# A new written order for a squared-ReLU attention and token/channel mixer kernel on one core

## The chip, the core and the metric

The kernel runs on one core of a Trainium2 chip. A core has five engines that run their own instruction streams and meet through semaphores: TensorE (PE, matrix products, and PEld, its weight loads), VectorE (DVE), ScalarE (ACT), GpSimd (POOL) and SyncE (SP). Data moves between memory and the core by DMA transfers; here POOL issues the loads of inputs and weights, and SP (at the end ACT too) issues the stores and the transposes that are done by DMA. Products land in PSUM, which has eight banks of 128 x 512 floats; everything else stands in SBUF. The metric is the device time of one execution in microseconds (us), lower being better.

## What is computed

Eight batches, twelve heads, 448 tokens, 64 numbers per head. The attention has no softmax: scores are clipped at zero and squared. Its output goes through a mixer over tokens and one over channels.

```python
def _attn_ref(q, k, v):                       # (8, 12, 448, 64)
    scores = scale * np.matmul(q, k.transpose(0, 1, 3, 2))
    attn = np.maximum(scores, 0.0) ** 2 / S
    return np.matmul(attn, v).astype(np.float32)
...
def _moe_ref(x, w_tok1, w_tok2, w_ch1, w_ch2):  # x (8, 448, 768)
    xt = x.transpose(0, 2, 1)
    h = np.maximum(xt @ w_tok1, 0.0) @ w_tok2   # 448 -> 256 -> 448
    u = x + h.transpose(0, 2, 1)
    h2 = np.maximum(u @ w_ch1, 0.0) @ w_ch2     # 768 -> 1536 -> 768
    return (u + h2).astype(np.float32)
```

## The kernel before

**Tiles.** The attention runs in 24 steps, three to a batch, four heads to a step; the four heads lie as two halves of two. Keys are cut into 7 tiles of 64 tokens. For every step the kernel does:

- `T`: PE transposes k and q against an identity matrix (line 472), 56 products of 64x64, one set for each half in steps 0 to 2 and further on partly for both halves; `cp` copies them out of PSUM (ACT or DVE, lines 349 and 351). From step 10 on, a crossing takes their place: DVE copies k and q, and SP transposes them by DMA (line 497).
- `S s.c`: the scores of key tile c, four products of 64x64 weights and 448 columns into two banks (line 515); `r` clips each bank into SBUF (ACT line 343 or DVE line 345), `q` squares both (ACT line 355 or DVE line 357).
- `V s.c`: the value products, again groups of four with 64x64 weights (line 542), summed over the seven tiles in two banks; `xe` empties these.
- The token mixer: `X` (PE transposes, line 579; from step 6 on SP does it by DMA, line 566), `t1` (line 588), its clipping `rt`, `t2` (line 597), and the addition `u` of x on DVE (line 601). These work on whole 128x128 tiles.

Per batch, `C1` (line 623) and `C2` (line 713) are the channel mixer of the earlier batches; `M1` (line 780) and `M2` (line 847) are products of pre-added weights and activations that take the place of some of its products, with additions and snapshots on DVE and ACT. SP transposes u into `u_sb` by DMA (`ub b.g`, line 610), six for each batch, and the last additions (`d2`, lines 860 and 862) read it before the stores `st` (line 668).

**Small and whole tiles.** `T`, `S` and `V` use PE as 64x64 tiles, all other products the whole 128x128 array. A run of small-tile operations between whole-tile ones is called a stretch here.

**Order.** Nothing is scheduled by a tool. All operations are built first, under names as above, and then issued one after the other as a table of words, `ORDER` (lines 73 to 242), says. A word is a name, and behind the colon stands what is left to choose: `:A` or `:D` sets ACT or DVE, digits set the PSUM banks of a product, and for a POOL load a name makes that load wait for another operation too. `fill:4*5` is a product of a zero tile whose result nothing reads, here one of 512 columns (5 // 4) and one of 128 (5 % 4) into bank 4. The order of the words is the order in which each engine meets its instructions.

```python
for word in ORDER.split():
    name, _, how = word.partition(':')
    ...
    o = self.ops[name]
    assert name not in done and all((d.name in done for d in o.deps)), name
    ...
    if how in ('A', 'D'):
        o.on = 'ACT' if how == 'A' else 'DVE'
    ...
    else:
        o.bank = [int(k) for k in how]
    o.emit(o)
```

**Loads.** POOL issues the halves of k, q and v (`ldk s.half` and so on, line 371, 112 KB each); a buffer is free again four steps later. The first q comes from SP and ACT (`ldf`, line 424) and is cast by DVE and ACT. The token weights are `wt1` and `wt2` (lines 382 and 389), the large channel weights `wc1.0` to `wc1.2` and `wc2.0` to `wc2.2` (lines 397 and 406), six parts of 768 KB. The identity matrix (`ident`, line 434) is made on POOL as well. The first two DMA transposes of u, `ub0.0` and `ub0.1`, are held until `wc2.2` has landed (`hold`).

Of the kernel before, what the change touches and what calls it, by code (L numbers as in the profile page):

```python
# [74 lines left out]
T0.0:0 ldv0.1 T0.1:1 cp0.0:D ldv0.0 cp0.1:D ldq2.0 ldk2.0 fill:4*5 S0.3:23
S0.1:45 S0.6:67 r0.3.0:A r0.3.1:D ldq2.1 S0.5:01 r0.1.0:A r0.1.1:D S0.0:23 wt1.1 r0.6.0:A r0.6.1:D r0.0.0:A
ldv1.1 q0.1:D r0.0.1:A ldk2.1 q0.3:D r0.5.0:A T1.0:45 r0.5.1:A q0.0:D S0.4:67 ldq3.0 S0.2:23 cp1.0:A cp1.1:D
ldk3.0 q0.5:D V0.0:01 r0.2.0:A S1.2:54 V0.1 q0.6:D r0.2.1:A ldv1.0 r0.4.0:A r0.4.1:D S1.3:23 ldv2.1 r1.2.0:A
q0.2:D r1.2.1:A wt1.0 q0.4:D r1.3.0:A V0.2 S1.1:67 ldv3.0 V0.3 q1.2:D r1.3.1:A V0.4 S1.4:54 r1.1.0:A ldk4.1
r1.1.1:D S1.0:23 r1.4.0:A r1.4.1:D ldk3.1 S1.6:67 r1.0.0:A V0.5 V0.6 q1.1:D r1.0.1:A ldk4.0 xe0.1:D xe0.0:A  # L80
ldq3.1 r1.6.0:A T2.0:54 q1.0:D r1.6.1:A q1.3:D X0.0:2 wt2 X0.1:3 cp2.0:A cp2.1:D S1.5:01 V1.0:67 ldq5.0 V1.1
q1.4:D r1.5.0:A V1.2 S2.3:45 ldq4.1 V1.3 r1.5.1:A xc0.0:D V1.4 xc0.1:D r2.3.0:A ldk5.1 S2.0:02 q1.5:D r2.3.1:A
S2.2:13 ldv4.0 q1.6:D r2.0.0:A fill:4*3 V1.5 S2.1:45 r2.0.1:A r2.2.0:D ldq6.1 r2.1.0:A r2.1.1:D S2.6:02 V1.6
ldv3.1 r2.2.1:A t1.0.0:1 q2.0:D xe1.0:A ldq5.1 S2.4:45 xe1.1:D r2.6.0:A V2.0:36 r2.6.1:A q2.1:D X1.1:0 ldq4.0
rt0.0:A q2.2:D r2.4.0:A fill:7*2 V2.1 S2.5:72 ldk6.0 q2.3:D r2.4.1:A V2.2 T3.0:14 r2.5.0:A xc1.1:D ldv5.0 V2.3
q2.4:D r2.5.1:A t2.0.0:5 cp3.0:A ldk5.0 cp3.1:D t1.1.1:0 X1.0:7 u0.0:D wc1.0 rt1.1:A V2.4 S3.2:24 xc1.0:A
q2.5:D t2.1.1:1 r3.2.0:A q2.6:D ldq6.0 S3.1:50 r3.2.1:A u1.1:D S3.4:72 ldk6.1 V2.5 r3.1.0:A V2.6 q3.2:D ub0.3
t1.1.0:4 r3.1.1:A ldv4.1 xe2.1:D xe2.0:A S3.0:15 wc1.2 t1.0.1:0 r3.4.0:A r3.4.1:D X2.1:6 rt1.0:A q3.1:D X2.0:3
r3.0.0:A wc2.0 S3.3:72 xc2.1:D rt0.1:A r3.0.1:A T4.0:41 xc2.0:D wc1.1 q3.4:D r3.3.0:A S3.6:60 t2.0.1:3
r3.3.1:A cp4.0:D t1.2.1:5 wc2.2 r3.6.0:A u0.1:D S3.5:72 r3.6.1:A cp4.1:D t1.2.0:4 rt2.1:A t2.1.0:6 r3.5.0:A  # L90
q3.0:D t2.2.1:3 rt2.0:A q3.3:D r3.5.1:A S4.1:05 S4.4:17 u1.0:D r4.1.0:A V3.0:42 V3.1 u2.1:D r4.1.1:A ub0.2
S4.3:60 V3.2 r4.4.0:A q3.5:D V3.3 S4.0:53 r4.4.1:A V3.4 r4.3.0:D ldk7.0 t2.2.0:1 r4.3.1:A ub0.5 q3.6:D V3.5
r4.0.0:A T5.0:76 u2.0:D r4.0.1:A ldq7.0 S4.2:05 V3.6 q4.1:D cp5.0:A ub0.4 C1.0.3:1 ldk7.1 xe3.1:D xe3.0:A
cp5.1:D ldv5.1 r4.2.0:A C1.0.1a:3 q4.0:D r4.2.1:A c1e0.3:A q4.3:D S4.6:72 S4.5:46 V4.0:05 q4.2:D r4.6.0:A V4.1
C1.0.1 r4.5.0:A r4.5.1:D C1.0.2a:1 r4.6.1:A q4.4:D c1e0.1:A C1.0.2 q4.5:D T6.0:74 q4.6:D c1e0.2:A S5.5:62 V4.2
cp6.0:A cp6.1:D V4.3 V4.4 ldq7.1 V4.5 r5.5.0:D S5.3:31 r5.5.1:A V4.6 S6.3:47 r5.3.0:A r5.3.1:D X3.0:6 xe4.0:A
xe4.1:D C1.0.9:2 r6.3.0:A r6.3.1:D xc3.0:A q5.3:D C1.0.10:3 q5.5:D c1e0.9:A q6.3:D wc2.1 X4.0:1 c1e0.10:A
S6.0:05 xc4.0:D S6.4:47 S6.1:62 r6.0.0:A C1.0.11:3 r6.0.1:A r6.4.0:D r6.1.0:A r6.4.1:D r6.1.1:A S5.4:10 q6.0:D
S5.6:54 c1e0.11:A S5.2:67 q6.1:D t1.4.0:2 r5.4.0:A q6.4:D r5.4.1:A t1.3.0:3 r5.6.0:A r5.2.0:D r5.6.1:A
r5.2.1:D ldv7.1 C1.0.8:1 rt4.0:A q5.4:D rt3.0:A q5.2:D S5.1:05 q5.6:D c1e0.8:A S6.5:64 w1.0.0:D S5.0:72  # L100
r5.1.1:D C1.0.5:3 r5.0.1:A r5.0.0:A w1.0.2:D r5.1.0:A t2.4.1:1 C1.0.6:2 u4.1:D ub0.1 ldq9.1 w1.1.0:D t2.3.1:5
c1e0.5:D c1e0.6:A C1.0.4:7 q5.1:D ub0.0 u3.1:D C1.0.7:0 c1e0.4:A q5.0:A C1.0.0a:1 c1e0.7:D C1.0.0 T7.0:32
c1e0.0:A V5.0:57 V5.1 cp7.0:A ldq8.0:ub0.1 V5.2 r6.5.1:D S6.2:01 V5.3 ldq8.1:ub0.1 cp7.1:D V5.4 r6.5.0:A V5.5
S6.6:43 ldk8.0 V5.6 w2.0.1:D M2.0.0.2:2 xe5.0:A ldk8.1 xe5.1:A w2.0.0:D ldv6.1 r6.6.0:A S7.3:65 w2.1.1:D
X5.0:7 r6.6.1:A ldv6.0 t2.3.0:4 w1.0.1:D xc5.0:A ldk9.1 M2.0.0.1:3 u3.0:D r6.2.1:A d2.0.0.11a:D t1.5.0:7
r7.3.1:A h0.0.0:D r6.2.0:A r7.3.0:D t2.4.0:4 rt5.0:A w2.1.0:D S7.4:12 S7.0:50 r7.4.1:A M2.0.0.5:6 h0.0.1:D
q6.5:A d2.0.0.11b:D ldk9.0:ub0.1 t2.5.1:7 r7.0.1:D q6.2:A t2.5.0:2 ldq9.0:ub0.1 u5.1:D M2.0.0.6 r7.0.0:A
ldq10.0 u4.0:D r7.4.0:A u5.0:D ldq10.1:ub0.1 C2.0.2.0:0 w2.3.1:D ldk10.1:ub0.0 d2.0.0.12a:D ldv7.0 w2.2.1:D
C1.1.0:7 ldk10.0 h0.0.2:D ldv8.0 w2.3.0:D T8.0:54 c1e1.0:A h0.2.s:D S7.1:12 q7.0:A cp8.1:D ldq12.1 M2.0.0.7
d2.0.0.22a:D ldk11.0 q6.6:A w2.2.0:D C2.0.2.1:7 ldk11.1 cp8.0:A c2e0.2.0:D ldk12.0 d2.0.0.22b:D q7.4:A ldq11.0  # L110
w1.1.2:D M2.0.0.4 ldq11.1 h0.0.3:D iq10:A c2e0.2.1:D ldq12.0 r7.1.0:D T9.0:40 d2.0.0.21:D S7.2:57 cp9.0:A
M2.0.0.3 cp9.1:D r7.2.0:D r7.2.1:A S8.0:13 r7.1.1:A ik10:D V6.0:04 V6.1 V6.2 d2.0.0.12b:D S7.6:75 V6.3
r8.0.1:A V6.4 r8.0.0:D V6.5 q7.3:A S7.5:26 q7.2:D V6.6 xk10 C1.1.2:3 xe6.1:A xe6.0:D r7.6.0:A r7.5.0:D
r7.6.1:A C1.1.1:1 w1.3.2:D xd6 q7.1:A r7.5.1:D c1e1.2:D S8.1:40 c1e1.1:A S8.6:72 st1.64 V7.0:56 q7.5:D
r8.1.0:A V7.1 V7.2 xq10 V7.3 r8.6.1:A q7.6:D V7.4 S8.5:31 r8.6.0:A r8.1.1:D V7.5 S9.0:42 r8.5.1:A V7.6
w1.1.1:D C1.1.4:7 xe7.1:A st2.0 xe7.0:D r9.0.1:A ldv9.0:xd6 r9.0.0:D r8.5.0:A xd7 C1.1.9:0 c1e1.4:A w1.3.1:D
ldv8.1 q8.5:A q8.0:D S8.3:16 ik11:D st0.64 S8.4:52 q9.0:A S8.2:43 c1e1.9:D C1.1.6:7 iq11:D r8.3.0:A
ldv9.1:st2.0 r8.4.0:A w1.3.0:D xq11 t1.6.0:0 ldk12.1:st1.64 q8.1:A r8.2.1:D r8.3.1:D C1.1.10:1 c1e1.6:A
rt6.0:D xk11 r8.2.0:A r8.4.1:A S9.4:53 S9.2:67 S9.1:04 r9.4.1:D ldq13.1:xd7 r9.2.1:A ub1.0 C1.1.5:2 r9.4.0:D
r9.2.0:A iq12:A q8.4:D t2.6.0:3 q9.4:D ub1.2 C1.1.3:7 q8.2:A u6.0:D q8.3:D c1e1.10:A t1.7.0:5 st1.0 c1e1.5:A  # L120
r9.1.0:D ldk13.1:xq11 r9.1.1:A ub1.5 q8.6:D V8.0:63 S9.5:12 rt7.0:D V8.1 V8.2 r9.5.0:A V8.3 c1e1.3:D S9.6:04
q9.1:A ub1.1 V8.4 V8.5 ldk14.0:xk11 ik12:D S9.3:51 V8.6 r9.6.1:D C1.1.11:7 xe8.0:A q9.2:D xe8.1:A r9.3.1:A
r9.6.0:D C1.1.8:4 xd8 r9.3.0:A ldk13.0:st1.0 r9.5.1:A ldq13.0:st1.0 q9.3:A t2.6.1:6 q9.5:D ub1.3 C1.1.7:3
# [880 lines left out]
```

## Time and profile before

| what | value |
|---|---|
| median of three runs | 346.44 us (345.43 to 347.01) |
| the profiled execution | 345.03 us |
| its span in the profile | 343.2 us |
| mean granted clock of PE | 0.993 |
| dearest group of DVE | L357, the squares, 105 of 620 ns, 62.0 us |
| dearest group of ACT | L343, the clippings, 238 of 570 ns, 117.3 us |
| POOL busy | 91.8 us |
| bytes moved | 50.19 MB, 146 GB/s on average |

The span runs from the first to the last instruction that the profile shows; the rest of the execution's time lies around it. In a timeline each row gives the start in us, the duration of the group, the engine, the line, the operation, what it writes and reads, and how many instructions. The ends of products are modelled, so that starts are the safer numbers. A row of a stretch gives its bounds and its length, and then the busy time of the engines.

### The profile page before, as it was taken

Reading aid. Unit: us, or ns where it says so; the run is one execution under the profiler, and the core shown is the slowest. Engines: PE = TensorE matmul, PEld = TensorE weight load, DVE = VectorE, ACT = ScalarE, POOL = GpSimd, SP = SyncE. Lnnn points to the kernel's source line nnn. Section 1 sums busy time; section 2 is a strip of 40 time slices with the busy share of each in tenths; the row PEclk is TensorE's granted clock in tenths of the full one; section 3 lists DMA queues with packets and bytes.
Section 4 is the critical chain, followed back from the end, with each engine's and each line's share of the span. In section 5 each row is a group of like instructions: output and inputs, shape, how many; then the busy total and the mean of one; then the engine's idle time right before and its main releaser. Section 6 shows DMA issues by size and latency. Waiting matters only on the chain.

```text
span 343.2 us, 9395 instructions
## 1 busy us (share of the span) xinstructions
PE 334.0 (97%) x3792; PEld 217.5 (63%) x3792; DVE 296.7 (86%) x577; ACT 242.5 (71%) x456; POOL 91.8 (27%) x157
## 2 busy tenths in 40 slices
PE   7799999999999999999999999999999999999995
PEld 3456455555555557675777655786579787787762
DVE  4999998799988999899979999899897886877763
ACT  3999986868998797999799986978974633031000
POOL 8986211383221371222811233200002000000000
PEclk9899999999999999999999999999999999999999
DMA  8999999798999999999999999996459032241464
GB/s 139 188 188 180 154 183 207 122 168 130 173 178 133 217 158 159 205 173 182 169 189 173 178 157 217 155 186 130 80 112 129 19 79 32 48 114 38 109 160 139
DMA packets 98939, 50.19 MB, mean 146 GB/s; under 512 B 71568, under 2 KB 95952, under 8 KB 98896
## 3 DMA queue, kind: packets, MB, share of 16 engines
q1 hardware_dynamic: 72736, 26.92, 45.3%
q0 software_dynamic: 25136, 21.47, 45.2%
q10 hardware_dynamic: 1024, 1.21, 1.2%
q8 instruction: 29, 0.48, 0.6%
q14 instruction: 14, 0.11, 0.1%
HBM read 43.38 MB, written 11.01 MB: 159 GB/s over the span
## 4 chain that ended last, share of the span: by engine, by line
PE 89%; DMA 3%; DVE 3%; SPq 3%; issue 0%; DVEq 0%; POOLq 0%
PE m_ps L847 24%; PE m_ps L780 22%; PE sc_ps L515 10%; PE acc_ps L542 9%; PE m_ps L623 6%; PE t_ps L588 6%; PE h_ps L597 5%; PE m_ps L713 5%; DMA u_sb<-uT 2%; SPq L610 2%; PE kqT_ps L472 1%; DVE arena L357 1%; DMA arena<-in_k_dram 1%; SPq L497 1%; PE x_ps L579 1%; DVE arena L345 1%
## 5 line engine op out<-in xcount | busy, mean ns | idle before, releaser
L343 ACT ACTIVATE arena<-sc_ps 128x448 bf16<-128x448 f32 x238 | 117.3, 570 | 14.8 <-PE sc_ps L515 13.4
L345 DVE TENSOR_SCALAR arena<-sc_ps 128x448 bf16<-128x448 f32 x98 | 59.4, 619 | 5.1 <-PE sc_ps L515 3.1
L357 DVE TENSOR_TENSOR arena<-arena 128x896 bf16<-128x896 bf16 x105 | 62.0, 620 | 1.0 <-ACT arena L343 0.9
L355 ACT ACTIVATE arena<-arena 128x896 bf16<-128x896 bf16 x63 | 58.5, 960 | 0.1
L371 POOL DMA_DIRECT2D arena<-in_v_dram x48 | 29.2, 618 | 98.0 <-PE m_ps L780 20.2
L515 PE MATMUL sc_ps<-arena 64*64 64x448 bf16 x672 | 54.2, 362 | 0.4
L542 PE MATMUL acc_ps<-arena 64*64 64x448 bf16 x672 | 46.4, 358 | 1.7 <-DVE arena L357 1.6
L780 PEld LDWEIGHTS <-wc 128*128 128x128 bf16 x432 | 40.8, 98 | 6.1 <-issue 3.2
L371 POOL DMA_DIRECT2D arena<-in_q_dram x46 | 28.1, 618 | 44.6 <-DMA u_sb<-uT 8.0
L371 POOL DMA_DIRECT2D arena<-in_k_dram x48 | 29.5, 620 | 21.2 <-DMA out_dram<-out_sb 9.4
L780 PEld LDWEIGHTS <-ws 128*128 128x128 bf16 x324 | 30.5, 98 | 4.5 <-issue 2.5
L515 PEld LDWEIGHTS <-arena 64*64 64x64 bf16 x672 | 19.7, 106 | 20.5 <-issue 13.6
L601 DVE TENSOR_TENSOR uT<-h_ps,xT 128x448 bf16<-128x448 f32 x48 | 29.1, 619 | 1.7 <-PE h_ps L597 1.5
L847 PE MATMUL m_ps<-wc,r 128*128 128x384 bf16 x162 | 30.3, 327 | 0.0
L542 PEld LDWEIGHTS <-arena 64*64 64x64 bf16 x672 | 20.6, 108 | 15.3 <-issue 5.3
L623 PE MATMUL m_ps<-uT,wc 128*128 128x448 bf16 x144 | 30.1, 353 | 0.0
L847 PEld LDWEIGHTS <-r 128*128 128x128 bf16 x216 | 20.2, 98 | 15.1 <-issue 3.1
L793 ACT ACTIVATE arena<-m_ps 128x448 f32<-128x448 f32 x18 | 9.4, 545 | 24.7 <-PE m_ps L780 7.6
L597 PE MATMUL h_ps<-wt,r_sb 128*128 128x448 bf16 x96 | 25.4, 353 | 0.0
L588 PE MATMUL t_ps<-x_sb,wt 128*128 128x256 bf16 (+1 forms) x216 | 25.4, 261 | 0.0
L780 PE MATMUL m_ps<-uT,wc 128*128 128x224 bf16 x216 | 25.0, 259 | 0.0
L847 PEld LDWEIGHTS <-sums 128*128 128x128 bf16 x180 | 17.3, 98 | 12.0 <-issue 1.3
(86 smaller groups left out, 507.2 us busy)
## 6 DMA issues: line engine op xcount, KB each, us to landing
out_dram<-out_sb SPq DMA_DIRECT2D x42, 192.0 KB, 3.7
arena<-in_k_dram POOLq DMA_DIRECT2D x48, 112.0 KB, 4.6
arena<-in_v_dram POOLq DMA_DIRECT2D x48, 112.0 KB, 4.6
arena<-in_q_dram POOLq DMA_DIRECT2D x46, 112.0 KB, 4.7
wc<-in_moe_w_ch_dram POOLq DMA_DIRECT2D x6, 768.0 KB, 16.9
out_dram<-arena SPq DMA_DIRECT2D x4, 192.0 KB, 2.8
out_dram<-out_sb ACTq DMA_DIRECT2D x8, 96.0 KB, 2.4
out_dram<-out_sb SPq DMA_DIRECT2D x8, 96.0 KB, 2.1
```

What stands on the lines that cost most here:

```text
L343: nc.scalar.activation(out, ps, AF.Relu)
L345: nc.vector.tensor_scalar(out=out, in0=ps, scalar1=0.0, scalar2=None, op0=ALU.max)
L355: nc.scalar.activation(x, x, AF.Square)
L357: nc.vector.tensor_tensor(out=x, in0=x, in1=x, op=ALU.mult)
L371: o.ins = nc.gpsimd.dma_start(out=raws[t][s % NR][64 * half:64 * (half + 1)], in_=src[b, h0:h0 + 2].rearrange('e (p c) d -> p e (c d)', c=KC))
L515: nc.tensor.matmul(o.ps[e][64 * half:64 * (half + 1), :S], lhsT=lhsT, rhs=rhs, start=True, stop=True, skip_group_check=True)
L542: nc.tensor.matmul(o.ps[half][64 * e:64 * (e + 1), :S], lhsT=r[rows, e, c * D:(c + 1) * D], rhs=sq[rows, e, :], start=c == 0, stop=c == KC ...
L588: nc.tensor.matmul(o.ps[:, j, :], lhsT=wt1[:, c, j * 128:(j + 1) * 128], rhs=x_sb[:, p0:p1, c, :], start=c == 0, stop=c == 3)
L597: nc.tensor.matmul(o.ps[:, :S], lhsT=r1[:, j, a * 128:(a + 1) * 128], rhs=wt2[:, j, :], start=j == 0, stop=j == JC - 1)
L623: nc.tensor.matmul(ps[:, :S], lhsT=wc1[:, g, e * 128:(e + 1) * 128], rhs=uT[:, g, off:off + S], start=g == 0, stop=g == CC - 1)
L780: nc.tensor.matmul(o.ps[:, j * HB:(j + 1) * HB], lhsT=lhs[:, g, (e + j) * 128:(e + j + 1) * 128], rhs=rhs[:, g], start=j == g == 0 and not ...
L847: nc.tensor.matmul(o.ps[:, :HN], lhsT=lhs[:, e], rhs=rhs[:, e], start=e == 0 and not on, stop=e == EC // 2 - 1, skip_group_check=True)
```

## The change

All of the table `ORDER` is written anew; nothing else is. The operations are the same, with the same operands. What differs is where each stands in its engine's stream, which PSUM banks the products take, whether ACT or DVE does a clipping, copy or square (ACT squares 76 of 168 tiles, before 63, and clips 232 score banks, before 238), and the fills (four in place of three). There are 52 stretches of small tiles, before 68. The first line of the table, before and now:

```diff
 ORDER = """
-ldf.0 ldf.1 ldk0.0 ldk0.1 ident ldk1.0 ldv2.0 cast0.0:D cast0.1:A ldq1.0 ldk1.1 cast1.0:D cast1.1:A ldq1.1
+fill:5*6 ldf.0 fill:4*4 fill:0*6 ident ldf.1 ldk0.1 ldk0.0 ldq2.1 ldq1.1 ldq1.0 ldk1.0 cast1.0:D cast1.1:A
...
```

On POOL, the start of the program. Its first rows before (`arena` holds k, q and v; the three rows of `masks.py` make the identity):

```order
L371 DMA arena_69<-in_k_dram 64x2x448 x2
masks.py:197 MEMSET ident_63 128x128
masks.py:199 ISA
masks.py:199 AFFINE_SELECT ident_63<-ident_63 128x128
L371 DMA arena_69<-in_k_dram 64x2x448
L371 DMA arena_69<-in_v_dram 64x2x448
L371 DMA arena_69<-in_q_dram 64x2x448
```

And now:

```order
masks.py:197 MEMSET ident_63 128x128
masks.py:199 ISA
masks.py:199 AFFINE_SELECT ident_63<-ident_63 128x128
L371 DMA arena_69<-in_k_dram 64x2x448 x2
L371 DMA arena_69<-in_q_dram 64x2x448 x3
L371 DMA arena_69<-in_k_dram 64x2x448 x2
L371 DMA arena_69<-in_v_dram 64x2x448
```

The identity stands ahead of the two loads of step 0's k, and the second half of k ahead of the first.

On POOL again, the large weights, before:

```order
L397 DMA wc1_67<-in_moe_w_ch1_dram 128x6x512
L406 DMA wc2_68<-in_moe_w_ch2_dram 128x4x768
L397 DMA wc1_67<-in_moe_w_ch1_dram 128x6x512
L406 DMA wc2_68<-in_moe_w_ch2_dram 128x4x768
L371 DMA arena_69<-in_k_dram 64x2x448
L371 DMA arena_69<-in_q_dram 64x2x448
L371 DMA arena_69<-in_k_dram 64x2x448
L371 DMA arena_69<-in_v_dram 64x2x448
L371 DMA arena_69<-in_q_dram 64x2x448
L406 DMA wc2_68<-in_moe_w_ch2_dram 128x4x768
L371 DMA arena_69<-in_v_dram 64x2x448
L371 DMA arena_69<-in_q_dram 64x2x448 x3
```

And now, from the third of the six parts on (`wc1.1`; `wc1.0` and `wc1.2` stand further ahead):

```order
L397 DMA wc1_67<-in_moe_w_ch1_dram 128x6x512
L371 DMA arena_69<-in_k_dram 64x2x448
L406 DMA wc2_68<-in_moe_w_ch2_dram 128x4x768
L371 DMA arena_69<-in_q_dram 64x2x448
L406 DMA wc2_68<-in_moe_w_ch2_dram 128x4x768
L371 DMA arena_69<-in_v_dram 64x2x448
L406 DMA wc2_68<-in_moe_w_ch2_dram 128x4x768
L371 DMA arena_69<-in_k_dram 64x2x448
L371 DMA arena_69<-in_v_dram 64x2x448
L371 DMA arena_69<-in_q_dram 64x2x448
```

Before, these were `wc1.2`, `wc2.0`, `wc1.1` and `wc2.2` together, then five loads that end with `ldq7.1`, the last of step 7's k and q halves, and then the sixth part, `wc2.1`. Now one load stands between each two of the last parts, `wc2.2` is the sixth, and `ldq7.1` (the last row here) follows it.

On PE, the end of step 3's value products, before (L542 value products, L597 the token mixer's second product):

```order
L542 LDWEIGHTS arena_69
L542 MATMUL acc_ps_938<-arena_69 64x448
L597 LDWEIGHTS r1_sb_72
L597 MATMUL h_ps_979<-wt2_66,r1_sb_72 128x448
L597 LDWEIGHTS r1_sb_72
L597 MATMUL h_ps_979<-wt2_66,r1_sb_72 128x448
L542 LDWEIGHTS arena_69
L542 MATMUL acc_ps_937<-arena_69 64x448
```

And now (L515 scores of step 4):

```order
L542 LDWEIGHTS arena_69
L542 MATMUL acc_ps_952<-arena_69 64x448
L515 LDWEIGHTS arena_69
L515 MATMUL sc_ps_981<-arena_69 64x448
L515 LDWEIGHTS arena_69
L515 MATMUL sc_ps_982<-arena_69 64x448
```

The whole-tile product that stood between two value groups is gone from there, and a score group of the same small tiles stands in its place.

On SP, the six transposes of batch 0's u stand together as before, but in another order: before `ub0.3`, `ub0.2`, `ub0.5`, `ub0.4`, `ub0.1`, `ub0.0`; now `ub0.1`, `ub0.0`, `ub0.2`, `ub0.5`, `ub0.3`, `ub0.4`.

More of the change, by code (lines that the diff above doesn't have):

```diff
@@ L73 @@
 ORDER = """
-ldf.0 ldf.1 ldk0.0 ldk0.1 ident ldk1.0 ldv2.0 cast0.0:D cast0.1:A ldq1.0 ldk1.1 cast1.0:D cast1.1:A ldq1.1
[L75 to L123, printed above, removed]
@@ new lines @@
+r4.2.1:A q3.6:D r4.4.0:A V3.2 V3.3 V3.4 V3.5 u2.1:D S4.5:13 V3.6 r4.5.1:A q4.2:D S4.6:74 xe3.1:A C1.0.2
+r4.6.1:D r4.5.0:A C1.0.3:3 r4.6.0:D c1e0.2:A ldq7.0 xe3.0:D r4.4.1:A S4.1:04 c1e0.3:D S4.0:17 T5.0:25 r4.1.0:A
+wc2.1 r4.0.1:D q4.6:A S4.3:63 C1.0.10:0 cp5.1:D r4.3.1:A cp5.0:D q4.5:D r4.1.1:A X3.0:7 r4.0.0:A q4.1:A
+xc3.0:D C1.0.1a:5 C1.0.1 q4.0:D ldv5.0 c1e0.10:A t1.3.0:3 r4.3.0:D c1e0.1:A wc2.2 q4.4:A q4.3:D ldk7.0 S5.3:24
+S5.1:17 V4.0:06 r5.1.0:A V4.1 r5.3.1:D V4.2 V4.3 rt3.0:A r5.3.0:D V4.4 V4.5 r5.1.1:A V4.6 S5.0:54 S5.6:12
```

280 lines of the change are left out of this document (162 added, 118 removed).

## The prediction

> **What bounds the kernel now.** I read the page first: its busy shares (first row), two rows of its 40 slices, and its shares of the chain of waits (last row).
>
> ```profile
> PE 334.0 (97%) x3792; PEld 217.5 (63%) x3792; DVE 296.7 (86%) x577; ACT 242.5 (71%) x456; POOL 91.8 (27%) x157
> PE   7799999999999999999999999999999999999995
> DVE  4999998799988999899979999899897886877763
> ACT  3999986868998797999799986978974633031000
> PE 89%; DMA 3%; DVE 3%; SPq 3%; issue 0%; DVEq 0%; POOLq 0%
> ```
>
> TensorE is busy for 97% of 343.2 us and makes 89% of the chain that ends last. But a share is an average, so I next cut the span into stretches.
>
> ```profile
> 10.50:14.00 3.50, 1.85 (x24) 0.62 (x17) 3.50 (x8) 3.50 (x9) 3.40 (x6) 1.00 1.24 184
> 14.00:17.40 3.40, 3.27 (x38) 2.18 (x41) 2.85 (x6) 2.78 (x7) 3.07 (x6) 0.54 1.26 190
> 31.00:38.40 7.40, 7.40 (x200) 4.33 (x201) 7.40 (x16) 7.40 (x19) 2.44 (x4) 1.00 1.33 163
> 38.40:64.00 25.60, 25.60 (x351) 13.71 (x343) 22.36 (x42) 20.79 (x41) 3.13 (x5) 1.00 1.21 190
> 64.00:128.00 64.00, 63.85 (x686) 34.93 (x687) 59.83 (x118) 55.43 (x97) 27.24 (x46) 1.00 1.09 158
> 128.00:177.00 49.00, 49.00 (x548) 32.64 (x540) 46.90 (x93) 42.81 (x80) 16.73 (x28) 1.00 1.19 177
> ```
>
> The columns are length, then PE, PEld, DVE, ACT, POOL busy, the clock, DMA, GB/s. From 10.5 to 14 us DVE and ACT are full and PE works 1.85 of 3.5 us: **the first 38 us are bound by DVE and ACT**, which empty the score banks. In the window after, the clock is 0.54. From 38.4 us on PE has no idle time to speak of (0.15 us in 64 to 128): **from there the time is what PE has to do**, with DVE at 93 to 96% behind it.
>
> **Term 1: fewer changes between small and whole tiles.** The timeline of PE, by start, duration and count:
>
> ```profile
> 90.28 0.76 PE L515 MATMUL sc_ps<-arena 64*64 64x448 bf16 x12
> 90.97 1.31 PE L623 MATMUL m_ps<-uT,wc 128*128 128x448 bf16 x6
> 92.12 1.04 PE L588 MATMUL t_ps<-x_sb,wt 128*128 128x256 bf16 x8
> 92.99 1.30 PE L623 MATMUL m_ps<-uT,wc 128*128 128x448 bf16 x6
> 94.22 0.76 PE L515 MATMUL sc_ps<-arena 64*64 64x448 bf16 x12
> 94.91 1.31 PE L623 MATMUL m_ps<-uT,wc 128*128 128x448 bf16 x6
> 96.06 0.54 PE L597 MATMUL h_ps<-wt,r_sb 128*128 128x448 bf16 x2
> 96.44 1.30 PE L623 MATMUL m_ps<-uT,wc 128*128 128x448 bf16 x6
> 97.57 0.60 PE L588 MATMUL t_ps<-x_sb,wt 128*128 128x256 bf16 x4
> ```
>
> Ends are modelled, so I use starts. Six L623 matmuls between whole-tile work take 97.57 - 96.44 = 1.13 us; before a small stretch 94.22 - 92.99 = 1.23; after one 96.06 - 94.91 = 1.15. Three score groups take 94.91 - 94.22 = 0.69 us. What three groups cost without a change I read from a long run:
>
> ```profile
> 222.53 1.49 PE L542 MATMUL acc_ps<-arena 64*64 64x448 bf16 x28
> 223.86 0.55 PE L515 MATMUL sc_ps<-arena 64*64 64x448 bf16 x8
> ```
>
> Seven groups of four in 223.86 - 222.53 = 1.33 us are 0.19 each, three 0.57. So a small stretch costs 0.10 us on entry and 0.12 + 0.02 on leaving; 0.21 us is the value I take (ends 0.19 and 0.24). Sixteen stretches fewer would be 3.4 us, if PE bounds everywhere. It doesn't in the first 38 us, so I count from the last value product of step 3 (the L542 group before the first L623 in the row at 38.76 below): 13 of 68 stretches stand ahead of it before, 9 of 52 now. Behind it 55 become 43: 12 x 0.21 = **-2.5 us** (ends -2.3 and -2.9). All other PE work behind that point is the same but for a group or two that crossed it.
>
> **Term 2: the fills.** Three fills (7 instructions, 128 to 512 columns) stand ahead of the first transposes now, and one (three of 512, two of 128 columns) among the scores of steps 0 and 1. A 448-column step is 0.19 us, so 512 are 0.22 and 128 are 0.05 by width: 0.9 us ahead and 0.76 within. The cover is PE's idle time in rows that follow: 0.93 us before the first transpose, and 1.65 us between 10.5 and 14. I cost them at 0; without that cover they cost 0.8.
>
> **Term 3: the first 38 us.** The timeline at the start, in brackets the idle time ahead of a group and its releaser; then single groups of ACT, DVE and PE further on:
>
> ```profile
> 1.24 1.32 POOL L371 DMA_DIRECT2D arena<-in_k_dram  x2 [0.80 <-POOLq L988]
> 2.54 0.24 POOL masks.py:197 MEMSET ident<- 128x128 bf16 x1
> 3.10 0.61 POOL L371 DMA_DIRECT2D arena<-in_k_dram  x1
> 5.63 1.20 PE L472 MATMUL kqT_ps<-ident,arena 64*64 64x64 bf16 x56 [0.93 <-DMA arena<-in_k_dram]
> 6.33 1.17 DVE L351 COPY arena<-kqT_ps 128x896 bf16<-128x896 bf16 x2
> ...
> 28.19 1.86 ACT L343 ACTIVATE arena<-sc_ps 128x448 bf16<-128x448 f32 x4
> ...
> 38.42 0.41 PE L542 MATMUL acc_ps<-arena 64*64 64x448 bf16 x4
> 38.76 0.55 PE L623 MATMUL m_ps<-uT,wc 128*128 128x448 bf16 x2
> ...
> 42.27 1.70 DVE L357 TENSOR_TENSOR arena<-arena 128x896 bf16<-128x896 bf16 x3
> ```
>
> The identity (3.10 - 2.54 = 0.56 us of POOL) now stands ahead of the first k load, and the half that PE transposes first is the second one loaded (0.6 us of issue). The first transpose is 0.3 to 1.2 us later; the two copies behind it, 1.17 us one after the other on DVE, now lie side by side on ACT and DVE and give about half a microsecond back. I take +0.3. Then the counts up to the last value product of step 3. DVE: 61 instructions before, 59 now, of which 56 and 53 at (1.70 - 0.62)/2 = 0.54 us and the others short: 1.3 us less. ACT: 57 evictions before and 51 now at (1.86 - 0.57)/3 = 0.43 us (0.57 and 0.62 are the single instruction), but two squares and two copies more at about 0.83: 0.4 us more. By these sums DVE was the longer with 32 us, and now both stand near 31. That is -1.0, with the start -0.7; I take **-0.5** (ends -1.2 and +1.0). The half-clock window I keep: the PE idle time ahead of it comes from DVE and ACT, and the fill within the scores is 0.76 of 1.65 us. Were it gone, DVE, busy 2.85 of 3.40 us in it, would gain up to 0.55, so the low end is -1.75.
>
> **Term 4: the weights that now stand ahead of step 7.** The six parts of the large weights were spread, the last behind both halves of step 7's k and q; now all six stand ahead of the last of those halves (ldq7.1), which the transposes of step 7 need. The timeline of POOL's issues and of PE's transposes:
>
> ```profile
> 25.83 0.86 POOL L397 DMA_DIRECT2D wc<-in_moe_w_ch_dram  x1
> ...
> 43.89 0.59 POOL L371 DMA_DIRECT2D arena<-in_q_dram  x1 [4.70 <-DMA wc<-in_moe_w_ch_dram]
> ...
> 47.88 0.76 POOL L406 DMA_DIRECT2D wc<-in_moe_w_ch_dram  x1 [3.40 <-DMA wc<-in_moe_w_ch_dram]
> ...
> 53.14 0.59 POOL L371 DMA_DIRECT2D arena<-in_v_dram  x1 [4.50 <-DMA wc<-in_moe_w_ch_dram]
> ...
> 56.97 0.59 POOL L371 DMA_DIRECT2D arena<-in_q_dram  x1 [3.24 <-DMA wc<-in_moe_w_ch_dram]
> ...
> 61.46 0.64 PE L472 MATMUL kqT_ps<-ident,arena 64*64 64x64 bf16 x56
> ```
>
> And the times from issue to landing, first of the part at 25.83, then of the six transposes of SP at L610 (batch 0):
>
> ```profile
> DMA to landing us min/median/max: 8.5/8.5/8.5
> ...
> DMA to landing us min/median/max: 7.5/9.2/13.0
> ```
>
> POOL is released by one part's landing after the other: 3.99, 5.26 and 3.83 us apart, 4.36 on average. The first part is POOL's 35th operation now instead of the 39th, 2.4 us earlier: issue 23.4, landing 31.9 with its 8.5. Five parts more (21.8) and twelve loads at 0.6 (7.2) bring ldq7.1 to 60.9 us; by 3.83 a part to 58.3, by 5.26 to 65.4. PE reaches that transpose at 61.46 before. Now it is 0.5 us earlier by term 3 and 1 us earlier by five stretches saved in all; three score groups and a transposition more, one L623 group less stand ahead: 60.5. So I take **+0.2** (ends 0 and +4.9). Of the six L610 transposes four ran beside the weights, and now all six follow the last part. Those that wait for `wc2.2`, `ub0.1` and `ub0.0`, stood last in SP's queue before and stand first now, ahead of the other four.
>
> The Trainium skill, "DMA: Bandwidth & Descriptors", section "Queues, rings and completion order", says that each DMA engine takes turns between the queues it has work for, so transfers aren't served strictly as issued over two queues. The trace agrees as far as it goes: the 5.26 is the part beside which transposes were in flight. By that rule, with none beside the weights now, 3.83 would hold, this term be 0 and the sum below -3.0.
>
> **The end.** The order closes as before with a product on PE, one DVE addition and a store on each of two queues:
>
> ```profile
> 338.98 0.56 DVE L860 TENSOR_TENSOR out_sb<-arena,m_ps 128x384 f32<-128x384 bf16 x1 [0.42 <-PE m_ps L847]
> ```
>
> From its end at 339.5 to the span's end it is 3.7 us, and I leave that.
>
> **Sum.** -2.5 - 0.5 + 0.2 = -2.8 us. The profiled execution took 345.03 us around its span of 343.2, so 342.2 would be its like. The median of the three runs, 346.44, is 1.4 above it, and the forecast is for that: **343.6 us**, 0.8% less.
>
> **Rivals.** *Weights late (slower).* If each part takes the 5.26 of the one slow spacing, ldq7.1 lands at 65.4, PE waits 4.9 us at step 7's transposes, and the sum is -2.5 - 0.5 + 4.9 = +1.9: 348.3 us. It decides above 4.9 us a part. For it: six heavy parts in one queue. Against: two of three spacings are below 4. The Trainium skill, "TensorE: Matmul & The Clock Gate", Part 1, says that an idle window of about 3.4 us halves the clock for the next; the 0.54 behind the half-idle window agrees. By that rule this rival would cost up to 1.7 us more, 350.0.
>
> *Transposes late.* The first additions of the second layer need the third of the six L610 transposes. Issued 1.25 us apart from the last part's landing (about 59), with 9.2 us to land it comes at 70.7, while PE needs the bank that these additions free at about 69: +2 us, 345.6. With 7.5 it costs nothing.
>
> *The start gains nothing.* Its end at +1.0 instead of -0.5: 345.1. For it: a late first transpose moves all that DVE and ACT do.
>
> *The saved changes turn into waits.* DVE is busy 59.83 of 64 us and 46.90 of 49; if PE, quicker by 2.5, finds banks full, most of it is lost: 346. Against it: DVE's total falls, since 13 squares and more go to ACT, which has room (71%).
>
> **Chances.** Forecast 0.51, late weights 0.16, late transposes 0.10, the start 0.16, waits 0.07. Half a per cent, 1.7 us, is about what a measurement tells from nothing: faster 0.51; within it 0.33 (transposes, start, waits); slower 0.16. The range starts below the sum of the good ends (-2.9 - 1.75, 341.8) by some of the scatter of the runs, 341.3, and reaches over the middle cases to 347.8, leaving out most of late weights.
>
> **What would show it.** A small stretch still 0.21 us; PE's idle time after 38 us below 1 us; the last value product of step 3 at 37 to 38 us; step 7's transposes at 60 to 61.5 us without a DMA as releaser. Wrong would be a gap in front of those transposes, DVE waiting for u_sb near 68 us, or a second window at half clock.

## The result

The changed kernel takes **345.22 us** (median of 20 runs, 342.48 to 348.53) where the kernel before takes 347.04 (20 runs, 344.89 to 351.58): a ratio of **0.9944, interval 0.9917 to 0.9970**, 0.56% or 1.9 us less. The ratio leaves out executions more than 1.5% above the fastest of their kernel (the medians, which hold all of them, differ by 1.8 us). The forecast was 343.6 for a kernel before at 346.44, 0.8% or 2.8 us less. The direction was right and the time lies in the range; the forecast gain was half again the measured one.

The two profiled executions say something else. The changed kernel was profiled in an execution of 346.45 us with a span of 344.4, above its median, and the kernel before in one of 345.03 with a span of 343.2, below its own. By the two traces alone the change costs 1.2 us. The experiments had to settle which of the differences between the traces belong to the order and which to the execution.

### The profile page after: what moved, and what is told of

Read it like the earlier page. It is cut to its first block, busy times and chain, and to the rows that moved or that the text cites. A ratio compares the mean times of both kernels' runs of the same rounds, so it can differ in the third digit from the quotient of the medians.

```text
span 344.4 us, 9413 instructions
## 1 busy us (share of the span) xinstructions
PE 333.3 (97%) x3796; PEld 222.5 (65%) x3797; DVE 295.0 (86%) x571; ACT 250.0 (73%) x462; POOL 92.3 (27%) x157
## 4 chain that ended last, share of the span: by engine, by line
PE 86%; DMA 6%; POOL 3%; DVE 2%; ACT 1%; issue 0%; POOLq 0%; ACTq 0%; DVEq 0%
PE m_ps L847 24%; PE m_ps L780 18%; PE sc_ps L515 10%; PE acc_ps L542 8%; PE m_ps L623 8%; PE t_ps L588 6%; PE h_ps L597 5%; PE m_ps L713 5%; DMA x_sb<-xT 4%; POOL arena L371 2%; DMA arena<-in_k_dram 2%; PE kqT_ps L472 1%; DMA arena<-in_q_dram 1%; PE x_ps L579 1%; DVE arena L796 1%; DVE uT L601 1%
## 5 line engine op out<-in xcount | busy, mean ns | idle before, releaser
L355 ACT ACTIVATE arena<-arena 128x896 bf16<-128x896 bf16 x76 | 72.4, 970 | 0.6 <-DVE arena L345 0.3
L345 DVE TENSOR_SCALAR arena<-sc_ps 128x448 bf16<-128x448 f32 x104 | 62.1, 616 | 3.9 <-PE sc_ps L515 3.5
L357 DVE TENSOR_TENSOR arena<-arena 128x896 bf16<-128x896 bf16 x92 | 55.1, 615 | 1.1 <-ACT arena L343 0.6
L515 PE MATMUL sc_ps<-arena 64*64 64x448 bf16 x672 | 54.2, 357 | 1.5 <-ACT arena L349 1.2
L542 PE MATMUL acc_ps<-arena 64*64 64x448 bf16 x672 | 42.7, 350 | 0.2
L515 PEld LDWEIGHTS <-arena 64*64 64x64 bf16 x672 | 22.0, 105 | 22.5 <-issue 13.8
L623 PE MATMUL m_ps<-uT,wc 128*128 128x448 bf16 x144 | 29.9, 353 | 0.0
L542 PEld LDWEIGHTS <-arena 64*64 64x64 bf16 x672 | 20.9, 106 | 11.3 <-issue 3.1
L796 DVE CUSTOM_DVE_ANT_0 r<-r,m_ps 128x448 bf16<-128x448 f32 x32 | 19.6, 616 | 8.8 <-PE m_ps L780 3.7
L597 PE MATMUL h_ps<-wt,r_sb 128*128 128x448 bf16 x96 | 25.1, 353 | 0.0
```

The costliest lines, as they stand in the source:

```text
L345: nc.vector.tensor_scalar(out=out, in0=ps, scalar1=0.0, scalar2=None, op0=ALU.max)
L355: nc.scalar.activation(x, x, AF.Square)
L357: nc.vector.tensor_tensor(out=x, in0=x, in1=x, op=ALU.mult)
L515: nc.tensor.matmul(o.ps[e][64 * half:64 * (half + 1), :S], lhsT=lhsT, rhs=rhs, start=True, stop=True, skip_group_check=True)
L542: nc.tensor.matmul(o.ps[half][64 * e:64 * (e + 1), :S], lhsT=r[rows, e, c * D:(c + 1) * D], rhs=sq[rows, e, :], start=c == 0, stop=c == KC ...
L597: nc.tensor.matmul(o.ps[:, :S], lhsT=r1[:, j, a * 128:(a + 1) * 128], rhs=wt2[:, j, :], start=j == 0, stop=j == JC - 1)
```

## The profile after

The page of the changed kernel: busy shares, two of the 40-slice rows, and the chain of waits.

```profile
PE 333.3 (97%) x3796; PEld 222.5 (65%) x3797; DVE 295.0 (86%) x571; ACT 250.0 (73%) x462; POOL 92.3 (27%) x157
PE   7899999999999999699999999999999999999995
DMA  8999999989999999999999998796676113432255
PE 86%; DMA 6%; POOL 3%; DVE 2%; ACT 1%; issue 0%; POOLq 0%; ACTq 0%; DVEq 0%
```

TensorE is as busy as before, but its row has a hole (the 6, in the slice that begins at 138 us), and DMA has 6% of the chain where it had 3%. The DMA engines are at 90% or more in most slices up to 207 us. The stretches cut as for the prediction (length, then PE, PEld, DVE, ACT and POOL busy, the clock, DMA, GB/s):

```profile
10.50:14.00 3.50, 2.82 (x90) 1.58 (x94) 3.35 (x7) 3.50 (x9) 2.80 (x5) 1.00 1.23 187
14.00:17.40 3.40, 3.28 (x94) 1.74 (x90) 3.40 (x7) 3.40 (x9) 3.40 (x7) 1.00 1.25 194
38.40:64.00 25.60, 25.57 (x405) 14.69 (x403) 21.86 (x40) 25.13 (x47) 7.86 (x14) 1.00 1.14 183
64.00:128.00 64.00, 64.00 (x698) 36.30 (x700) 61.43 (x122) 53.78 (x97) 25.24 (x43) 1.00 1.12 163
128.00:177.00 49.00, 45.92 (x502) 32.84 (x494) 43.92 (x87) 42.95 (x80) 14.73 (x25) 1.00 1.34 166
```

DVE and ACT still fill the stretches up to 38 us, the half clock of 14.0 to 17.4 us is gone, and in 128 to 177 us TensorE idles for 3.08 us, where it idled for none before. The timeline of PE shows the places that the prediction named, and the hole:

```profile
37.86 0.47 PE L542 MATMUL acc_ps<-arena 64*64 64x448 bf16 x4
...
61.50 0.65 PE L472 MATMUL kqT_ps<-ident,arena 64*64 64x64 bf16 x56
...
140.89 1.05 PE L588 MATMUL t_ps<-x_sb,wt 128*128 128x256 bf16 x8 [3.08 <-DMA x_sb<-xT]
```

The last value product of step 3 comes at 37.86 us (38.42 before), step 7's transposes at 61.50 without a wait (61.46), and at 140.89 the token mixer of step 10 has waited 3.08 us for its transposed x. SP's timeline shows that transpose third in a row of three:

```profile
125.77 1.18 SPq L610 DMA_TRANSPOSE u_sb<-uT  x1
127.05 1.39 SPq L497 DMA_TRANSPOSE arena<-arena  x1
128.53 3.05 SPq L566 DMA_TRANSPOSE x_sb<-xT  x1
```

It was ready to be issued at 124.5 us. SP issued it at 128.5, because the transpose of u in front of it waited for its input until 125.7, and it then took 12.3 us to land.

## The experiments

In the modified kernels line numbers can stand up to 3 higher or lower.

### The same kernel again

No edit.

> The changed kernel itself, to see which of its waits come back. In its first profile TensorE waited 3.1 us at 137.8 us for the transposed x of step 10, whose transfer took 12.3 us. If that wait belongs to the order (it stands third behind two other transposes in SP's queue), it returns, between 1 and 4 us. If it was an accident of one execution, TensorE is busy throughout from 128 to 177 us, as in the kernel before, and the span is about 341 us. Time: 0.5% under the kernel before by either.

343.89 us (median of 6 runs, 342.71 to 347.86), ratio 0.9925 (0.9869 to 0.9980). The transpose of step 10's x in this execution, by the view of its tile:

```profile
L566 SPq DMA_TRANSPOSE x_sb<-xT x1: 1842/1842/1842, 129.5 to 129.5; - x1
...
DMA to landing us min/median/max: 6.0/6.0/6.0
```

The same transpose, issued from the same place in the queue, takes 6.0 us where it took 12.3, and TensorE doesn't wait between 128 and 177 us; the span is 341.9. The wait is an event of the execution. What remains open is whether the order provokes it more often than the order before did.

### One transpose earlier

```diff
-M2.0.5.3 tu2.2:D ub2.5 ... xk14 ... V11.3 xd10
+M2.0.5.3 tu2.2:D xd10 ub2.5 ... xk14 ... V11.3
```

> The transpose of step 10's x is issued by SP ahead of two other transposes (the sixth of batch 2's u and step 14's k) that have 26 and 13 us to spare. By the theory of the queue it is issued at 124.5 us where it was 128.5, lands before 136, and the wait in front of step 10's token mixer is gone: 1 to 3 us less than the changed kernel in its first profile, 341 to 342.5 us of span. By the rival, that the DMA engines are simply full there, it takes 12 us from wherever it starts, lands at 136 to 137, and something behind it (step 14's scores, near 151) waits instead: no gain.

345.26 us (6 runs, 344.15 to 347.89), ratio 0.9968 (0.9921 to 1.0015), span 343.3. The transpose is issued at 124.5 us and takes 5.3, so it lands with 7.8 us to spare. TensorE's waits between 40 and 280 us (what it waited for; us in total, times, longest):

```profile
PE t_ps L588 <- DMA x_sb<-xT: 1.3, 1, 1.3
PE sc_ps L515 <- DVE out_sb L860: 0.6, 1, 0.6
```

The first is now step 12's x, the second a bank that DVE couldn't empty because the store that frees its output buffer was late. In this execution the wait stood elsewhere, as the rival had it, though the transfer took 5.3 us and not the rival's 12. One trace doesn't show that the edit moved it.

### What a small stretch costs

Behind 41 score groups that have small tiles on both sides stands one product of 64 columns with whole-tile weights:

```diff
+            if f'S{s}.{c}' in EXTRA:
+                nc.tensor.matmul(o.ps[0][:, S:S + 64], lhsT=ident, rhs=ident[:, :64], start=True, stop=True, skip_group_check=True)
```

> 41 products of 64 columns with whole-tile weights are put behind 41 score groups that have small-tile work on both sides: 41 changes into whole tiles and back, and 41 x 64 columns (0.03 us each by the 0.19 us of 448 columns). If a change there and back costs 0.21 us on TensorE, 41 x 0.24 = 9.8 us are added to the changed kernel (8 to 12). If it costs nothing, or is hidden, 1.2 us.

And the same 41 products behind second products of the token mixer, where whole-tile work follows:

```diff
+                    if f't2.{s}.{a}' in EXTRA:
+                        nc.tensor.matmul(o.ps[:, S:S + 64], lhsT=ident, rhs=ident[:, :64], start=True, stop=True, skip_group_check=True)
```

> The same 41 products of 64 columns, now behind 41 second products of the token mixer that have whole-tile work behind them, so that no stretch is added: 41 x 0.03 = 1.2 us by columns, up to 2.5 us if a short product costs 0.06. If the cost in the split kernel is that of the additional instructions and not of the change of tile, both kernels lose the same.

352.76 us with the products in small stretches (4 runs, 352.24 to 353.64; ratio 1.0177, 1.0126 to 1.0228), 343.83 with them in whole-tile work (4 runs, 343.60 to 348.75; 0.9951, 0.9881 to 1.0020). The difference is 8.9 us, or **0.22 us for each change there and back**. The second kernel has only four runs, one 5 us above the others. By the two traces, behind step 3's last value product and less TensorE's listed waits, it is 312.7 us against 304.6, or 0.20 for each. One of the changes in PE's timeline:

```profile
181.36 0.36 PE L516 MATMUL sc_ps<-arena 64*64 64x448 bf16 x4
181.65 0.20 PE L518 MATMUL sc_ps<-ident 128*128 128x64 bf16 x1
181.79 0.38 PE L545 MATMUL acc_ps<-arena 64*64 64x448 bf16 x4
```

A group of four takes 0.19 us when small tiles follow. Here 0.29 us pass before the whole-tile product starts and 0.14 before small tiles start again: 0.24 us added, the product's own time (0.03 by its columns) included. The Trainium skill, "TensorEngine Tiling (Array Packing)", section "Tiling Modes", says that a change of the tiling mode drains the engine. That a change costs time agrees with the runs, which give it this price.

The profiled execution of the second kernel was its slowest, 348.75 us, with more and longer waits than the first trace of the changed kernel:

```profile
PE t_ps L589 <- DMA x_sb<-xT: 2.2, 2, 1.9
PE sc_ps L516 <- DVE out_sb L863: 1.7, 1, 1.7
PE acc_ps L543 <- DMA arena<-in_v_dram: 0.7, 1, 0.7
```

All three stand between 120 and 159 us, and all three end in a transfer: the transposes of steps 10 and 12, a late store, a late v.

### SP in order of need

The 56 issues of SP between 103 and 201 us are put in the order in which their results are needed. The words of SP alone, from 110 us on:

```diff
-... xd9 xk12 xk13 ub2.2 ub2.4 xq13 st4.0 ub2.5 xk14 xd10 st4.64 xd11 ub3.1 xq14 ...
+... xd9 xk12 xk13 ub2.2 ub2.0 xq13 ub2.1 st4.0 st3.64 xd10 xk14 st3.0 ub2.4 ub2.5 xd11 xq14 ...
```

> SP's 56 issues between 103 and 201 us put in the order in which their results are needed (the two stores of tile 3 and the transposes of x, k and q ahead, stores and transposes of u that have 20 to 40 us to spare behind); nothing else is changed. In four profiles of the changed order TensorE waited between 106 and 177 us for 3.6, 0.5, 2.5 and 5.8 us, in front of step 10's and step 12's token mixer and for a bank that a late store held. If SP's order is the cause, these waits fall under 0.7 us, the median comes to 342.5 to 343.5 us and its scatter shrinks. If the DMA engines are simply full, one wait is traded for another: 344 to 346 us as for the changed kernel.

347.25 us (12 runs, 344.47 to 350.67), ratio 0.9997 (0.9952 to 1.0041): the gain of the whole change doesn't show any more, the median lies above what either theory had, and the scatter is no smaller. Waits of TensorE between 103 and 200 us:

```profile
PE sc_ps L512 <- DMA arena<-arena: 1.1, 1, 1.1
PE t_ps L585 <- DMA x_sb<-xT: 0.9, 1, 0.9
```

They end at 187 and 198 us now, where the first three traces of the changed order had none. SP's order has a part in who waits. That somebody waits seems to come from elsewhere.

### Without 18 stores

```diff
+                    if n < 14 and o.name not in GATES:
+                        return
                     o.ins = queue.dma_start(out=dst[..., cols], in_=out_sb[p, cols])
```

`GATES` holds the ten stores of these tiles behind which a load waits; they stay.

> The changed kernel without 18 of the 28 stores of output tiles 0 to 13 (3.5 MB; these rows of the output are not written), 11 of them between 103 and 201 us. If full DMA engines make the waits at 106 to 177 us, they are gone: under 0.5 us there, span about 341 us, all runs within 1 us of one another at 342.5 to 343.5. If the waits have another source (one slow transfer now and then), they and the scatter of 5 us stay.

343.65 us (6 runs, 342.72 to 344.25), ratio 0.9901 (0.9863 to 0.9940). TensorE has no wait between 103 and 200 us, and the span is 341.1. In a later set of runs the kernel before got the same treatment:

> The kernel before without the same 18 stores (these rows of the output are not written). If full DMA engines also make the scatter of the kernel before (344 to 352 us), it shrinks to about 1.5 us, and the pair of kernels without these stores shows what the written order alone is worth: by the counts of TensorE's work 2.5 us for the stretches, 0.5 us for the first 38 us, and about 0.8 us given back in small waits, so 2.1 to 2.3 us between the two. If the scatter of the kernel before has another source, it stays at 5 us or more.

> The changed kernel without the 18 stores again, beside the one of before in the same set of runs: 343 to 344 us, 2.1 to 2.3 us below it if the order is worth what its counts say, under 1 us below it if the gain measured on the whole kernels came from fewer waits for transfers.

The kernel before without these stores: 345.68 us (10 runs, 344.96 to 348.42; ratio 0.9992, 0.9953 to 1.0032). The changed kernel without them: 343.71 us (10 runs, 342.67 to 345.23; 0.9926, 0.9890 to 0.9962). Both scatter less (2.6 us for 6 in the changed kernel, 3.5 for 7 in the kernel before, though over 10 runs for 20 or more), so much of the scatter goes with these stores, and not all of it in the kernel before. Full DMA engines are the likely reason, but without the stores SP also has 18 issues fewer and the output buffers come free sooner, and no run tells these apart. In the second trace of the changed kernel without them TensorE has one wait of 0.5 us between 103 and 200 us, for a bank. The pair differs by **2.0 us**, near the 2.1 to 2.3 expected, but the agreement is partly luck: the trace of the kernel before holds a wait of 1.6 us for the weights (below), which the counts leave out and which these stores, all later, don't touch. The 1.2 us in the other direction between the first two traces was the 3.1 us wait.

### The fills and the clock

The four fills are taken out of the first lines of the table:

```diff
-fill:5*6 ldf.0 fill:4*4 fill:0*6 ident ...
+ldf.0 ident ...
-... S0.2:36 fill:0*14 r0.3.0:A ...
+... S0.2:36 r0.3.0:A ...
```

> The changed kernel without its four fills. By the prediction (their cost is hidden) the first transposes start where they did, at 6.2 to 6.9 us, since they wait for the first half of k that lands at 6.3, and the last value product of step 3 stands at 37.4 to 38.2 us as in four profiles with them. If the fills hold the first transposes up, these come 0.3 to 0.5 us earlier and so does all behind. If the fill among the scores is what keeps the clock at 1.00 near 14 us (it was 0.54 in the kernel before), a window of half clock returns there and the last value product of step 3 comes up to 0.55 us later.

And one fill more in the kernel before:

```diff
-ldk3.0 q0.5:D V0.0:01 ...
+ldk3.0 q0.5:D fill:0*14 V0.0:01 ...
```

> The kernel before with one fill more (three products of 512 columns and two of 128, 0.76 us) ahead of the first value product, in TensorE's idle time at 10.6 to 11.6 us. If PE's idle time there makes the half clock of 14.0 to 17.4 us, the clock stays above 0.9 now and the last value product of step 3 comes 0.2 to 0.6 us before 38.42. If not, clock and time stay. Behind that it is a second look at the kernel before: whether TensorE waits for transfers between 106 and 177 us there too (0.9 us in the first profile).

Each had one run: 343.75 us, and 346.50. Without fills the first transposes start at 6.22 us, as soon as k has landed. With fills they start at 6.53 to 6.85 in seven traces and at 6.17 in one. The start in the changed kernel, the landing of k's second half (issued at 2.15 us), then the one early start (the kernel with 41 whole-tile products), then the kernel without fills:

```profile
5.01 1.66 PE L970 MATMUL fill_ps<-out_sb 128*128 128x512 bf16 x7
6.60 0.97 PE L472 MATMUL kqT_ps<-ident,arena 64*64 64x64 bf16 x56
...
DMA to landing us min/median/max: 4.2/4.2/4.2
...
4.69 1.03 PE L973 MATMUL fill_ps<-out_sb 128*128 128x512 bf16 x7
6.17 0.97 PE L473 MATMUL kqT_ps<-ident,arena 64*64 64x64 bf16 x56 [0.45 <-DMA arena<-in_k_dram]
...
6.22 0.97 PE L472 MATMUL kqT_ps<-ident,arena 64*64 64x64 bf16 x56 [1.00 <-DMA arena<-in_k_dram]
```

So the fills do hold the transposes up. In the seven traces k had landed by 6.0 to 6.3 us, and the transposes follow the last fill without a wait for a transfer, 0.3 to 0.85 us after the landing. There the seven fills take 1.5 to 1.8 us by starts (6.60 - 5.01 = 1.59), where 0.9 was expected by width; in the one trace in which they take about 1.0, the transposes wait for k again. The delay isn't given back either: in all eight traces with these fills the last value product of step 3 starts 31.25 to 31.4 us behind the first transposes, at 37.43 to 38.23. Without fills it stands at 37.71, 31.49 behind them, and the clock did fall (windows of the kernel without fills):

```profile
7.00:10.50 3.50, 2.74 (x73) 1.71 (x69) 2.80 (x6) 2.95 (x6) 3.50 (x7) 0.76 1.20 176
10.50:14.00 3.50, 2.51 (x79) 1.37 (x75) 3.15 (x7) 3.37 (x8) 3.14 (x6) 0.50 1.25 187
14.00:17.40 3.40, 3.35 (x90) 2.08 (x79) 3.40 (x8) 3.40 (x8) 2.99 (x6) 0.76 1.24 193
```

By the distance of 31.49 us the half clock costs about 0.2 us here, since DVE and ACT, which bound this stage, keep most of their pace. So the fills have a price and a use, and taken out all together they show no gain at 38 us.

With its additional fill the kernel before keeps a clock of 1.00, and the last value product of step 3 stands at 38.35 for 38.42. That doesn't show the half clock to be hidden: in this execution TensorE stood still for 0.44 us at 36 us without a releaser that the profile knows, and without that the product could have come up to 0.44 earlier, inside the 0.2 to 0.6 expected. In the kernel before with later transposes (below) the clock is at 0.62 and 0.59 in two of these windows, and the product stands at 39.49. What the half clock costs in the kernel before stays open.

### The weights

The second trace of the kernel before (the one with the fill) brought something that the first had hidden. TensorE's waits there behind 40 us:

```profile
PE m_ps L847 <- DMA wc<-in_moe_w_ch_dram: 0.8, 1, 0.8
PE m_ps L847 <- DVE out_sb L862: 0.7, 1, 0.7
```

And in the third (without the 18 stores):

```profile
PE m_ps L850 <- DMA wc<-in_moe_w_ch_dram: 1.6, 1, 1.6
```

In the first trace that part of the weights, `wc2.1`, was just in time. By the view of its tile it was issued at 47.9 us and took 15.5, and by the timeline DVE's first sum of it starts at 63.50:

```profile
L406 POOL DMA_DIRECT2D wc<-in_moe_w_ch_dram x1: 764/764/764, 47.9 to 47.9; - x1
...
DMA to landing us min/median/max: 15.5/15.5/15.5
```

```profile
63.50 0.75 DVE L688 TENSOR_TENSOR ws<-wc 128x1152 bf16<-128x1152 bf16 x1
```

It landed at 63.4.

In the changed kernel the last of the six parts is issued at 39.2 us and takes 17.7, so all have landed by 56.9. One part of the change alone was tried in the kernel before: the four transposes of batch 0's u that ran beside the weights follow the two held ones.

```diff
-... q3.2:D ub0.3 ... r4.1.1:A ub0.2 ... r4.3.1:A ub0.5 ... cp5.0:A ub0.4 ... q5.1:D ub0.0 u3.1:D ...
+... q3.2:D ... r4.1.1:A ... r4.3.1:A ... cp5.0:A ... q5.1:D ub0.0 ub0.2 ub0.3 ub0.5 ub0.4 u3.1:D ...
```

> The kernel before with one part of the change alone: the four transposes of batch 0's u that SP issued at 29.5 to 38.7 us, beside the large weights, now stand behind the two that wait for wc2.2. In three profiles of the kernel before its sixth weight part, wc2.1, landed at 63.4, 64.4 and about 65 us, and TensorE waited for it 0.0, 0.8 and 1.6 us. If those transposes take time from the weights on the DMA engines, wc2.1 lands 2 to 4 us earlier, near 60 to 61.5, the wait is gone, and the median falls by about 1 us. By the rival that the weights come in their own queue's turn, wc2.1 still lands at 63 to 65 and the wait stays. By the rival of the prediction that late transposes hold up the second layer's additions, TensorE waits 1 to 2 us near 69 us instead.

346.16 us (12 runs, 344.14 to 348.44), ratio 0.9969 (0.9933 to 1.0005): about a microsecond, not clear of the scatter. The trace is clearer. The fifth part, `wc2.2`, in the kernel before and then in this one (issue; the largest landing time of its window is its own):

```profile
L406 POOL DMA_DIRECT2D wc<-in_moe_w_ch_dram x1: 828/828/828, 30.8 to 30.8; - x1
...
DMA to landing us min/median/max: 22.6/24.2/25.9
```

```profile
L406 POOL DMA_DIRECT2D wc<-in_moe_w_ch_dram x1: 842/842/842, 32.0 to 32.0; - x1
...
DMA to landing us min/median/max: 18.5/20.0/21.5
```

It is issued 1.2 us later and lands 3.2 earlier, at 53.5 for 56.7. `wc2.1` lands at 61.8 (46.1 + 15.7), and the wait for it is gone. TensorE doesn't wait near 69 us either, so the transposes were not late.

### A trimmed version

```diff
-fill:5*6 ldf.0 fill:4*4 fill:0*6 ident ldf.1 ldk0.1 ldk0.0 ...
+ldf.0 ident ldf.1 ldk0.1 ldk0.0 ...
-M1.7.0.3 ub7.0 M2.2.5.3 M2.2.5.7 d2.2.5.12b:D st19.64 M1.7.0.1:4 d2.2.5.22b:D M1.7.2.5:5 M1.6.4.7 tu7.2:D
+M1.6.4.7 M1.7.0.3 ub7.0 M2.2.5.3 M2.2.5.7 d2.2.5.12b:D st19.64 M1.7.0.1:4 d2.2.5.22b:D M1.7.2.5:5 tu7.2:D
```

> The changed kernel without the three fills ahead of the first transposes, and with one product (the fourth of batch 6's second sum) moved ahead of one that waits 0.56 us for a snapshot at 300 us. The fill among the scores stays. By the traces the first is worth 0.2 to 0.4 us in front of the last value product of step 3 (37.4 to 38.2 us with the fills), and the second 0.56 us at the end: 0.8 us less than the changed kernel, 0.7 to 0.8% below the kernel before. If the clock halves again without the leading fills, or the wait only moves to the next product, nothing is gained.

**343.04 us** (12 runs, 342.20 to 345.41), ratio 0.9901 (0.9865 to 0.9937): clearly below the kernel before, and below both medians of the changed kernel, though the intervals overlap. The wait that the second edit removes is in the changed kernel's timeline:

```profile
299.42 1.31 PE L780 MATMUL m_ps<-uT,wc 128*128 128x224 bf16 x12
301.13 0.54 PE L780 MATMUL m_ps<-uT,ws 128*128 128x224 bf16 x4 [0.40 <-ACT arena L793]
```

Twelve of these products take 1.15 us (six take 0.575 by their starts, 296.72 to 297.30 and further), so the next was due at 300.57 and came 0.56 late. It came so in all nine traces that keep this order. In the trimmed one the products follow one another there. The first edit shows no gain: k landed late in the trimmed trace (the first transposes start at 6.89 us), and the last value product of step 3 comes 32.2 us behind them, at 39.08, where it was 31.3 with the fills. TensorE is slower there: 24 score products that take 1.97 us in the second trace of the changed kernel (8.62 to 10.59) take 2.39 (8.86 to 11.25). The window rows have no loss of clock at that place; a halved clock would explain it, but isn't shown. How much of the 343.04 is the second edit and how much the set of runs isn't known, since the changed kernel wasn't run whole beside it.

## Why the prediction was right, and what it missed

The direction and the main mechanism were right: PE bounds the kernel behind the first 38 us, and fewer changes of tile save time there. That the sum came within 0.9 us is partly luck: the stretches saved less than forecast and the fills cost something, while the weights, counted as a small loss, were a gain.

**Term 1, the stretches (-2.5): the price right, the saving smaller.** The price of 0.21 us for each, read from starts, stands at 0.22 by times, 0.20 by the traces and 0.24 by starts (a short product included) in a kernel made for it. What the whole term saved can be read behind the last value product of step 3: the rest of the span less TensorE's listed waits. (The work that crossed this mark cancels: three score groups and a transposition went behind it, 1.0 us, and a score group and four L623 products came ahead of it, 0.95.) That is 343.2 - 38.4 = 304.8 us in the first trace of the kernel before and 304.6 to 305.2 in the others of its order; it is 344.4 - 37.9 - 3.5 = 303.0 in the first of the changed kernel and 302.8 to 303.9 in the others of its order that have no products added. So about 1.7 us were saved, outside the forecast's ends of 2.3 and 2.9. The other 0.8 came back in pieces that the list of waits doesn't show, among them this stretch of three score groups, which lasts 0.95 us where the prediction read 0.69:

```profile
49.67 1.01 PE L515 MATMUL sc_ps<-arena 64*64 64x448 bf16 x12
50.62 2.44 PE L623 MATMUL m_ps<-uT,wc 128*128 128x448 bf16 x12
```

The later expectation for the kernel before without the stores had 0.8 us of such small waits. What causes each of them stays open.

**Term 2, the fills (0): wrong by 0.3 to 0.85 us in seven of eight traces.** The cover that the prediction counted, TensorE's idle time ahead of the first transposes, was too short: the fills took 1.5 to 1.8 us and not 0.9, and the delay stays in the time at 38 us. What they do for the clock seems to pay part of it back. The forecast also kept the half-clock window; in the changed kernel it is gone.

**Term 3, the first 38 us (-0.5): right.** -0.56 between the first two traces. The first transposes came 1.0 us later (6.60 for 5.63), inside the 0.3 to 1.2, but about 0.3 of this is the fills and 0.7 the later landing of the k that they need. From there to the mark it is 31.3 us for 32.8 before, so the shorter work of DVE and ACT more than made up for it. (By the prediction's own figures ACT had 0.7 us more and not 0.4; the term hardly changes.) Over more executions the mark lies at 37.4 to 38.2 us in the eight traces that keep the start of the changed order, and at 38.4 to 39.5 in four of the order before. So the true term may be larger, although two of these four hold a standstill of 0.4 and 1.3 us and two a half clock.

**Term 4, the weights (+0.2, ends 0 and +4.9): the sign was wrong.** The landing of `ldq7.1` was right: 58.0 us (44.3 + 13.7), close to the 58.3 of the fastest of the three spacings, and step 7's transposes don't wait. What failed is the lower end of 0. Parts that stand earlier also land earlier, and `wc2.1` had 0.1 us to spare in the one trace that I read. In two more traces of the order before it came late, for 0.8 and 1.6 us, and this is what the change removes. That the spacing of 5.26 alone had transposes beside it was misread: one issued at 38.7 us took 13.0, so the spacing of 3.99 (43.9 to 47.9) had them too. The reason itself does hold: with no transposes beside the weights the fifth part landed 3.2 us earlier though it was issued 1.2 later. This agrees with the Trainium skill, "DMA: Bandwidth & Descriptors", section "Queues, rings and completion order", by which an engine takes turns between its queues.

**What no term held.** Two waits are new. The one of 0.56 us at 301 us belongs to the order and is in every trace that keeps it. The other, for transfers, mostly between 95 and 159 us, is an event of the execution: 3.1 us in the first trace of the changed order and none in its second. So TensorE's idle time behind 38 us was 3.5 us in the first, where the prediction's sign was under 1, and 0.4 in the second. A rival had DVE's banks as the new wait and priced it at 346. In three traces the wait did end at a bank that DVE had not emptied (0.5 to 1.7 us), but behind a late store; the others were for transfers themselves. The prediction had the DMA engines only as a number in a column (1.09 to 1.33) that it did not read.

Added up with the runs: -1.7 for the stretches, -0.5 to -0.9 at the start (the fills included), 0 to -1.6 at the weights, +0.4 for the snapshot (the part that the list of waits shows), and 0 to +3 for transfers. The measured -1.9 lies among these, but the range is too wide to confirm any one of them. What the waits for transfers cost on average in either kernel is open: that takes more traces than were taken.

**The rivals.** Late weights: refuted, the six parts land by 56.9 us. Late transposes: refuted, with all six behind the weights nothing waits for them. The start gains nothing: refuted by the marks at 38 us. Saved changes turn into waits: partly so, about 0.8 us in small pieces and 0.4 at the snapshot.
